# Fourteen products of 64 rows in place of three full ones and a half: a fused attention and MLP layer on one core

## The chip, the cores and the metric

The kernel runs on one core of one Trainium2 chip. The metric is the device time of one execution in microseconds; smaller is better. Of the kernel before there are three timed runs and one profiled execution.

## The reference

The layer computes two branches on the same normalised input, and adds both to the input:

```python
x = A_x                                  # [1, 2048, 448], bfloat16
xn = layernorm(x)
# branch A: linear attention with a feature map, 16 heads of 28
q, k, v = split_heads(xn @ wqkv)         # wqkv [448, 1344]
pq, pk = per_head(q @ w_phi), per_head(k @ w_phi)
phi_q = concat([softmax(pq), softmax(-pq)])
phi_k = concat([softmax(pk), softmax(-pk)])
kv = einsum("bhsf,bhsd->bhfd", phi_k, v);  z = phi_k.sum(over s)
o = (phi_q @ kv) / (phi_q . z + 1e-6)
# branch B: MLP with 1792 hidden features, mish(h) = h * tanh(softplus(h))
return x + o @ wo + mish(xn @ w1 + b1) @ w2
```

What matters here is that the model width is 448, which is three and a half times TensorE's 128 rows.

## The kernel before

The 2048 tokens are 16 tiles of 128, taken in 8 pairs u. For each pair the kernel normalises both tiles (bn_stats and bn_aggr on DVE in `st`, Ln and Exp on ACT, the scaling on POOL or DVE in `xn`) and transposes the result (`xt`, by DMA from SP or by TensorE). Each tile's 448 features give three chunks of 128 rows and one of 64; the two 64-row chunks of a pair share one block, one in rows 0 to 63 and the other in rows 64 to 127. So a transposed pair is 7 blocks in `xnT`.

Every product over the 448 features is built by `pair_part` (L376) for two results at once: part F is six products over 128 rows, three for each result, and part H is two products over 64 rows, one in each half of TensorE's array. F and H are separate steps and either may come first; the two PSUM banks of the pair are held from the first to the second. The units are v and k (8 each, 448 columns), q (2 x 4, 512 columns), f (the first MLP product, 2 x 14, 512 columns), and wo (8, 448 columns, L707, written out in the same way). The second MLP product g (L692) has 1792 rows, which is 14 full chunks, for each of 16 tiles.

Wq and Wk are first multiplied by w_phi: wtq and wtk transpose them on TensorE (L468), wmq and wmk multiply by a block-diagonal matrix `Wbd` (L481) that POOL builds with a mask, and ACT or DVE evicts the results into Wpq and Wpk. These steps run at the start, while the inputs load. TensorE first runs NWARM products on zeros.

After k, ACT takes two exponentials (L518), `kn` normalises them on DVE (L528, L530) and POOL (L532), and `kv` (L553) sums over tokens in column halves of the array. After all eight kv, `kvz` on DVE stores the sums for `nd` (L623), 16 small products of 56 rows in row halves for each tile, whose seven DVE instructions (L639 to L650) give o. `ot` transposes a pair of o by DMA for wo. f is evicted by ACT with the Mish function (L602), q by two exponentials (L588). ACT's function table is loaded with `ACT_TABLE_LOAD` whenever its function set changes.

The order of all steps is one hand-written list, `ORDER`. Each engine runs its own steps in that order, one after the other, and so does each DMA queue: an issue on SP that waits (for example `xt3m` for the normalised pair) holds back every later issue on SP. All buffers and PSUM banks are guarded by semaphores that `Program` derives from what each step reads and writes. A name in ORDER ends in the engine: a for ACT, d for DVE, p for POOL, s for a load issued by SP, m for a transpose by DMA.

Of the kernel before, what the change touches and what calls it, by code (L numbers as in the profile page):

```python
# [19 lines left out]
FC = F // P  # L20
G = 4
GP = 112
# [4 lines left out]
NWARM = 12  # L27
# [122 lines left out]
lx1s lpa lx0a lqta lkts bd lkms lbs lx2s table st1 st0 b1 wtk1d wtk0a lqms xn1p lvts lvms wmk1a xn0p st2 lx4s  # L150
wtq1d xt1d xn2p wmk0a wmq1a st3 wtq0d v1Hd k1H k1F xt0m st4 v1Fd wmq0a xn3p xn4p xt2m k0F v0Ha l1ts k0H k2H
kn1.0 st7 xt3m kn1.1 v0Fa v2Fa v2Ha kn0.1 q0.2H k2F q0.2F kn0.0 xt4m v4Fd st5 xn5p k3F kn2.1 kv1 v4Hd k3H k4F
kv0 k4H kn2.0 xn7d q0.0H q0.1H q0.1F kn3.0 l1ms xt5m q0.0F kn4.1 v3Fd k5F st6 kv2 v3Hd v5Ha xn6p k5H kn4.0 v5Fa
q0.3F xt7m k7H xt6m q0.3H k7F v7Fd kv4 kn3.1 kv3 kn5.1 v6Ha kn5.0 v7Hd v6Fa k6F k6H q1.0H kn7.0 q1.2H kn7.1
q1.0F q1.2F f1.3F l2s kn6.1 f0.7F f1.3H f0.7H kv5 kn6.0 kv7 kv6 f0.1F kvz f0.3F nd2 f1.2H f0.3H f0.1H f1.2F
q1.1F nd3 q1.1H nd1 los q1.3H q1.3F f0.4H f0.4F f0.8F f0.2F f0.5F f0.8H f0.2H f0.5H f1.1H f1.1F f1.4F f0.0F
f1.4H ot1m f0.0H f1.13H nd0 f1.13F f1.5F f1.7F f1.7H f1.6H nd7 f1.6F f1.10F ot0m f1.10H nd6 ot3m f1.5H f0.10H
f0.10F f1.0F nd5 f1.0H f0.6H f0.11H f0.6F f0.11F f1.12F nd4 f1.11H f1.12H nd10 f1.11F f0.13F f0.12F f0.12H ot2m
f0.13H nd8 f0.9H f0.9F f1.8F nd11 nd9 f1.8H wo0H g1 g0 wo0F ot5m wo3F nd14 wo3H nd15 ot7m f1.9H f1.9F g6 g7 g11
ot4m wo5H wo2H nd12 nd13 wo5F g5 wo4F wo2F sto3 g10 ot6m g4 g15 wo7H wo6H wo1H sto0 wo4H g8 wo7F wo6F g13 wo1F  # L160
stt15 g9 sto4 g12 g2 sto5 sto6 g3 sto2 sto1 g14 stt14
# [8 lines left out]
def _kernel(es, nc, A_x, A_wqkv, A_w_phi, A_wo, B_w1, B_b1, B_w2, out):  # L170
# [8 lines left out]
    mask = sb("mask", [GP, 4], FP32)  # L179
    Wraw = sb("Wraw", [GP, G, DH], BF16)  # L180
    Wbd = sb("Wbd", [GP, G, 2, 64], BF16)
# [10 lines left out]
    xn = [sb(f"xn{i}", [P, 2 * D], BF16) for i in range(NXN)]  # L192
    xnT = sb("xnT", [P, NU, 7, P], BF16)
    W1 = sb("W1", [P, 4, F], BF16)
    W2 = sb("W2", [P, FC, D], BF16)
    Wo = sb("Wo", [P, 7, D], BF16)
    Wv = sb("Wv", [P, 4, D], BF16)
    Wqk = [sb("Wq", [P, 4, D], BF16), sb("Wk", [P, 4, D], BF16)]
    Wp = [sb("Wpq", [P, 4, G * P], BF16), sb("Wpk", [P, 4, D], BF16)]
    WT = [sb(f"WT{i}", [GP, 2, G, P], BF16) for i in range(2)]  # L200
    actT = sb("actT", [P, FC, S], BF16)
    zeros = actT[:, 0, 0:TCW]
    NE = 3
# [11 lines left out]
    o_sb = [xn[i][:, :].rearrange("p (i d) -> p i d", i=2) for i in range(2)]  # L215

    def as_t(src):
# [4 lines left out]
    t2 = as_t(phik[0])  # L222


    oT_home = [(Wqk[1], [("Wk", i) for i in range(3)]), (Wqk[0], [("Wq", i) for i in range(3)]),
               (Wv, [("Wv", i) for i in range(3)]), (Wp[1], [("Wp", 1, h) for h in range(2)])]

    def oT_of(u):
        flat = oT_home[u // 2][0][:, :, :].rearrange("p c f -> p (c f)")
        return flat[:, (u % 2) * 7 * P:(u % 2 + 1) * 7 * P]  # L230
# [25 lines left out]
    def load_main(eng, name, dst, src):  # L256
        dma(eng, lambda e: e.dma_start(dst[:, 0:3, :], src[0:384, :].rearrange("(c p) f -> p c f", p=P)),  # L257
            w=[(name, 0)], tag="ld" + name)

    def load_tail(eng, name, dst, src):  # L260
        for i, (lo, hi) in enumerate(HALF):
            dma(eng, lambda e, lo=lo, hi=hi: e.dma_start(dst[lo:hi, 3, :], src[384:448, :]), w=[(name, 1 + i)],  # L262
                tag="ld" + name)

    def rows_of(name):
        return [(name, i) for i in range(3)]

    def load_phi(eng):
        dma(eng, lambda e: e.dma_start(Wraw[:], A_w_phi.rearrange("(g j) d f -> (j d) g f", j=4)), w=[("Wraw",)],
            tag="ldWphi")  # L270
# [4 lines left out]
    def load_w2(eng):  # L275
        dma(eng, lambda e: e.dma_start(W2[:], B_w2.rearrange("(c p) d -> p c d", p=P)), w=[("W2",)], tag="ldW2")

    def load_wo(eng):
        for n, (dst, src) in enumerate((
                (Wo[:, 0:3, :], A_wo[0:384, :].rearrange("(c p) d -> p c d", p=P)),  # L280
                (Wo[:, 4:7, :], A_wo[64:448, :].rearrange("(c p) d -> p c d", p=P)),
                (Wo[0:64, 3, :], A_wo[384:448, :]), (Wo[64:128, 3, :], A_wo[0:64, :]))):
            dma(eng, lambda e, dst=dst, src=src: e.dma_start(dst, src), w=[("Wo", n)], tag="ldWo")

    def table():
# [10 lines left out]
    op("POOL", lambda e: e.memset(mask[:], 1.0), w=[("mask",)])  # L296
    op("POOL", lambda e: e.affine_select(out=mask[:], in_=mask[:], compare_op=ALU.is_ge, fill=0.0, base=0,
                                         channel_multiplier=1, pattern=[[-DH, 4]]),
       r=[("mask",)], w=[("mask",)])
    op("POOL", lambda e: e.affine_select(out=mask[:], in_=mask[:], compare_op=ALU.is_ge, fill=0.0, base=DH - 1,  # L300
                                         channel_multiplier=-1, pattern=[[DH, 4]]),
       r=[("mask",)], w=[("mask",)])
    for i in range(NPH):
        op("POOL", lambda e, i=i: e.memset(v_ext[i][:, :, :, DH:DH + 1], 1.0), w=[("v1", i)])
    op("POOL", lambda e: e.memset(Wbd[:], 0.0), w=[("Wbd0",)])
# [54 lines left out]


    open_ = {}

    def pair_part(key, part, works, r, then):
        if key not in open_:
            open_[key] = take2()
            first = True
        else:
            first = False
        b = open_[key]  # L370

        def f(e):
            for o, par, lhs, rhs in works(b):
                for c in range(3) if part == "F" else (3,):
                    k = (0, P) if part == "F" else HALF[par]
                    ins = e.matmul(o, lhs(c, k), rhs(c, k), start=first and c in (0, 3), stop=not first and c in (2, 3))  # L376
            return ins
        pe(f, r, [pb(b), pb(b + 1)], key + part)
        if not first:
            then(b)  # L380
            free2(b)
# [22 lines left out]
    def ln_pair(u, eng):  # L404
        X = xn[u % NXN]
        a, b = 2 * u, 2 * u + 2
        if eng == "POOL":
            op("POOL", lambda e: e.tensor_tensor(shift[:, a:b], mv[:, a:b, 0], rstd[:, a:b], ALU.mult),
               r=[("mv", a), ("mv", a + 1), ("rstd", u)], w=[("sh", u)], tag=f"sh{u}")
            op("POOL", lambda e: e.tensor_scalar(shift[:, a:b], shift[:, a:b], -1.0, 0.0, op0=ALU.mult, op1=ALU.add),  # L410
               r=[("sh", u)], w=[("sh", u)], tag=f"sj{u}")
        for t in (a, a + 1):
            parts = [(0, D, 0)] if t % 2 == 0 else [(384, D, D), (0, 384, D + 64)]
            for n, (lo, hi, at) in enumerate(parts):
                if eng == "POOL":
                    op("POOL", lambda e, t=t, lo=lo, hi=hi, at=at: e.tensor_scalar(  # L416
                        X[:, at:at + hi - lo], x_all[:, t, lo:hi], rstd[:, t:t + 1], shift[:, t:t + 1],
                        op0=ALU.mult, op1=ALU.add),
                       r=[("x", t), ("sh", u), ("rstd", u)], w=[("xn", u % NXN, t % 2, n)], tag=f"xn{t}.{n}")
                else:  # L420
                    op("DVE", lambda e, t=t, lo=lo, hi=hi, at=at: e.tensor_scalar(  # L421
                        X[:, at:at + hi - lo], x_all[:, t, lo:hi], mv[:, t, 0:1], rstd[:, t:t + 1],
                        op0=ALU.subtract, op1=ALU.mult),
                       r=[("x", t), ("mv", t), ("rstd", u)], w=[("xn", u % NXN, t % 2, n)], tag=f"xn{t}.{n}")
# [12 lines left out]
    def xT(u, eng):  # L437
        i = u % NXN
        if eng == "DMA":
            dma("SP", lambda e: e.dma_start_transpose(xnT[:, u, :, :], xn[i][:, :]),  # L440
                r=[("xn", i, 0, 0), ("xn", i, 1, 0), ("xn", i, 1, 1)], w=[("xnT", u)], tag=f"xTm{u}")
            return
        b = take1()
        pe(lambda e: transpose7(e, b, xn[i]), [("xn", i, 0, 0), ("xn", i, 1, 0), ("xn", i, 1, 1), ("ident",)], [pb(b)],
# [6 lines left out]
    def w_bd():  # L451
        for r in range(2):
            op("POOL", lambda e, r=r: e.tensor_tensor(
                Wbd[:, :, r, 0:QP].rearrange("p g (j f) -> p g j f", f=DH),
                ap_on(Wraw[:, 0, 0:1], [[DH, G], [0, 2], [1, DH]]),
                ap_on(mask[:, 2 * r:2 * r + 1], [[0, G], [1, 2], [0, DH]]), ALU.mult),
               r=[("Wraw",), ("mask",), ("Wbd0",)], w=[("Wbd", r)], tag=f"Wbd{r}")
# [366 lines left out]
```

## Time and profile before

| | us |
|---|---|
| timed runs, median of 3 | 161.92 (161.06 to 162.26) |
| profiled execution | 162.46 |
| its span, first to last instruction | 160.7 |
| TensorE products (PE), busy | 152.4 |
| DVE, busy | 100.9 |
| ACT, busy | 75.6 |
| POOL, busy | 45.5 |

The page gives busy time and share of each engine, the span in 40 slices with the busy share of each in tenths, the clock that TensorE was granted, the DMA engines' share, and the chain of work that ended last. PE is a product on TensorE, PEld a load of its stationary weights, which runs beside products. In the rows of a timeline the columns are start, duration, engine, line, operation, tiles and count, and in brackets the idle time before and what ended it; rows of a PE group also hold the pipeline's tail, so that the start times of neighbours give the pace. The rows of a table of stretches hold the stretch, its length, the busy time (and instructions) of PE, PEld, DVE, ACT and POOL, the granted clock, the DMA engines' share and GB/s. TensorE ran 3.6 us of the first 15 at a clock of 0.53 and all else at about full clock. The DMA moved 12.96 MB in all.

### The profile page before, as it was taken

The page shows a single profiled execution, that of the slowest core. Times are in us where ns is not written, and L with a number is a line of the kernel's source. Part 1 is how long each engine was busy: PE and PEld are TensorE (multiplying, and loading weights), DVE is VectorE, ACT ScalarE, POOL GpSimd, SP SyncE. Part 2 cuts the span into 40 slices and gives each one's busy share as a digit, 9 for nine tenths or more (in the row PEclk, how much of TensorE's full clock was granted, in tenths as well). Part 3 has the DMA queues.
Part 4 walks back from the last instruction along what each step waited for, and adds up shares of the span by engine and source line. Part 5 has one row for each costly group of instructions (what it writes and reads, how often), then busy time and mean ns, then how long its engine had stood idle before and what let it go on. Part 6 is the DMA issues. An engine that isn't in the chain of part 4 may idle for free.

```text
span 160.7 us, 3100 instructions
## 1 busy us (share of the span) xinstructions
PE 152.4 (95%) x1300; PEld 74.5 (46%) x1300; DVE 100.9 (63%) x209; ACT 75.6 (47%) x91; POOL 45.5 (28%) x73
## 2 busy tenths in 40 slices
PE   6659999998999999999999999999999999999993
PEld 2346545453444544434444454454545554555551
DVE  1768799999968168910778589988928811311131
ACT  2355988895939949997668756300100000000000
POOL 6766699959989600000000000000000000000000
PEclk9996999999999999999999999999999999999999
DMA  5998948240498000200030203060070130000502
GB/s 146 284 354 129 183 76 324 40 81 2 70 329 259 8 0 4 57 0 0 4 57 0 57 4 57 0 61 0 2 168 8 23 91 0 0 33 0 225 4 86
DMA packets 21306, 12.96 MB, mean 81 GB/s; under 512 B 14892, under 2 KB 20524, under 8 KB 21292
## 3 DMA queue, kind: packets, MB, share of 16 engines
q1 hardware_dynamic: 20524, 12.39, 30.6%
q10 hardware_dynamic: 768, 0.37, 0.9%
q8 instruction: 10, 0.16, 0.4%
q14 instruction: 4, 0.03, 0.1%
HBM read 7.48 MB, written 1.84 MB: 58 GB/s over the span
## 4 chain that ended last, share of the span: by engine, by line
PE 82%; POOL 5%; DVE 5%; DMA 4%; SPq 2%; issue 1%
PE PS L376 41%; PE PS L692 27%; PE PS L707 7%; POOL phik L532 4%; DMA Wq<-in_A_wqkv_dram 4%; PE PS L623 3%; DVE xn L421 2%; PE PS L553 2%; PE PS L481 1%; DVE Sk L528 1%; POOL xn L416 1%; PE PS L468 1%; SPq L262 1%; DVE v_ext L435 1%; SPq L257 0%
## 5 line engine op out<-in xcount | busy, mean ns | idle before, releaser
L376 PE MATMUL PS<-xnT,W 128*128 128x512 bf16 (+1 forms) x224 | 45.9, 379 | 0.0
L692 PE MATMUL PS<-W,actT 128*128 128x448 bf16 x224 | 43.5, 353 | 0.0
L602 ACT ACTIVATE actT<-PS,b1T 128x1024 bf16<-128x1024 f32 x28 | 30.0, 1112 | 21.3 <-PE PS L376 21.3
L692 PEld LDWEIGHTS PS<-W,actT 128*128 128x128 bf16 x224 | 21.8, 98 | 20.9 <-issue 0.8
L376 PEld LDWEIGHTS PS<-xnT,W 128*128 128x128 bf16 (+1 forms) x224 | 17.5, 97 | 23.4 <-issue 4.9
L532 POOL TENSOR_TENSOR phik<-Ek,rSk 128x896 bf16<-128x896 bf16 x16 | 26.8, 1699 | 2.6 <-DVE rSk L530 2.5
L682 DVE TENSOR_TENSOR x_all<-PS,x_all 128x448 bf16<-128x448 f32 x16 | 9.8, 622 | 25.8 <-PE PS L692 24.6
L528 DVE TENSOR_REDUCE Sk<-Ek 128x32 f32<-128x896 bf16 x16 | 16.8, 1050 | 0.6 <-ACT Ek L518 0.6
L588 ACT ACTIVATE EqT<-PS 128x1024 bf16<-128x1024 f32 x16 | 15.2, 1030 | 0.4 <-PE PS L376 0.2
L518 ACT ACTIVATE Ek<-PS 128x896 bf16<-128x896 f32 x16 | 13.8, 915 | 3.3 <-PE PS L376 3.2
L376 PE MATMUL PS<-xnT,Wpq 128*128 128x512 bf16 (+1 forms) x64 | 13.9, 379 | 0.7 <-DVE v_ext L435 0.7
L639 DVE COPY Sq<-PS 128x16 f32<-128x16 f32 x32 | 4.0, 168 | 16.7 <-PE PS L623 16.5
L376 PE MATMUL PS<-Wpk,xnT 128*128 128x448 bf16 (+1 forms) x64 | 13.0, 356 | 0.0
L376 PE MATMUL PS<-Wv,xnT 128*128 128x448 bf16 (+1 forms) x64 | 12.9, 360 | 0.0
L416 POOL TENSOR_SCALAR xn<-x_all,rstd,shift 128x448 bf16<-128x448 bf16 (+2 forms) x21 | 12.1, 589 | 0.7
L395 DVE BATCH_NORM_STATS2 stats<-x_all 128x6 f32<-128x448 bf16 x16 | 9.5, 596 | 3.3 <-DMA x_all<-in_A_x_dram 3.3
L647 DVE TENSOR_TENSOR Ek<-Ek,phik 128x464 f32<-128x464 f32 x16 | 10.3, 642 | 0.6
L643 DVE TENSOR_TENSOR Ek<-PS,Sq 128x464 f32<-128x464 f32 x16 | 10.3, 642 | 0.5
L650 DVE TENSOR_TENSOR xn<-Ek,rden 128x448 bf16<-128x448 f32 x16 | 10.0, 625 | 0.6
L645 DVE TENSOR_TENSOR phik<-PS,Sq 128x464 f32<-128x464 f32 x16 | 10.1, 631 | 0.0
L376 PEld LDWEIGHTS PS<-xnT,Wpq 128*128 128x128 bf16 (+1 forms) x64 | 5.2, 97 | 7.0 <-DVE v_ext L435 1.1
L376 PEld LDWEIGHTS PS<-Wpk,xnT 128*128 128x128 bf16 (+1 forms) x64 | 5.1, 97 | 6.3 <-issue 2.1
(64 smaller groups left out, 111.7 us busy)
## 6 DMA issues: line engine op xcount, KB each, us to landing
W<-in_B_w_dram SPq DMA_DIRECT2D x1, 1568.0 KB, 8.8
out_dram<-x_all SPq DMA_DIRECT2D x7, 224.0 KB, 2.1
W<-in_B_w_dram SPq DMA_DIRECT2D x1, 1344.0 KB, 6.2
x_all<-in_A_x_dram SPq DMA_DIRECT2D x1, 896.0 KB, 7.3
Wo<-in_A_wo_dram SPq DMA_DIRECT2D x2, 336.0 KB, 9.3
x_all<-in_A_x_dram SPq DMA_DIRECT2D x1, 448.0 KB, 5.4
W<-in_B_w_dram SPq DMA_DIRECT2D x2, 224.0 KB, 4.1
Wk<-in_A_wqkv_dram SPq DMA_DIRECT2D x1, 336.0 KB, 4.4
```

What stands on the lines that cost most here:

```text
L376: ins = e.matmul(o, lhs(c, k), rhs(c, k), start=first and c in (0, 3), stop=not first and c in (2, 3))
L416: op("POOL", lambda e, t=t, lo=lo, hi=hi, at=at: e.tensor_scalar(X[:, at:at + hi - lo], x_all[:, t, lo:hi], rstd[:, t:t + 1], shift[:, t:t ...
L518: op("ACT", lambda e, s=s: e.activation(Ek[i][:, s, :, :], two(b, D), ACT.Exp, scale=1.0 if s == 0 else -1.0), r=[pb(b), pb(b + 1)], w=[(" ...
L528: op("DVE", lambda e: e.tensor_reduce(Sk[i][:, s, :], Eh(), AX.X, ALU.add), r=[("Ek", i, s)], w=[("Sk", i, s)], tag=f"Sk{u}.{s}")
L532: op("POOL", lambda e: e.tensor_tensor(phik[j][:, s, :, :].rearrange("p i (h f) -> p (i h) f", f=DH), Eh(), ap_on(rSk[i][:, s, 0:1], [[1, ...
L588: op("ACT", lambda e, s=s: e.activation(EqT[:, s, g, q * 1024:(q + 1) * 1024], bank(b, 2), ACT.Exp, scale=1.0 if s == 0 else -1.0), r=[pb( ...
L602: op("ACT", lambda e: e.activation(actT[:, fc, q * 1024:(q + 1) * 1024], bank(b, 2), ACT.Mish, bias=b1T[:, fc:fc + 1]), r=[("b1T",), pb(b) ...
L643: op("DVE", lambda e: e.tensor_tensor(tv(t1[i]), num(0), sx(1), ALU.mult), r=[pb(b), pb(b + 1), ("Sq", i, 1)], w=[("t1", i)], tag=f"ta{t}")
L645: op("DVE", lambda e: e.tensor_tensor(tv(t2), num(1), sx(0), ALU.mult), r=[pb(b), pb(b + 1), ("Sq", i, 0)], w=[("t2",)], tag=f"tb{t}")
L647: op("DVE", lambda e: e.tensor_tensor(t1[i], t1[i], t2, ALU.add), r=[("t1", i), ("t2",)], w=[("t1", i)], tag=f"tc{t}")
L692: ins = e.matmul(bank(b)[:, 0:D], actT[:, fc, tok(t)], W2[:, fc, :], start=first and fc == 0, stop=last and fc == FC - 1)
L707: ins = e.matmul(bank(b)[:, 0:D], oT_of(u)[lo:hi, cc * P:(cc + 1) * P], Wo[lo:hi, cc, :], start=first and c in (0, 3), stop=last and c in ...
```

## The change

All products over 448 rows become 14 products of 64 rows, seven for each of the two results, which alternate between the upper and lower half of the array. F and H are one step, `pair_mm`, and the banks are no longer held between parts. To serve both halves, each transposed block now holds the same 64 features of both tiles of a pair, one tile in each half, and every weight (Wv, W1, Wo, Wpq, Wpk) lies in both halves: Wv, W1 and Wo are loaded twice, once into each half, by two DMA steps; Wpk is computed in both halves (56 products over 64-column halves for wmk, 16 before for one copy); Wpq is computed once into Wqn and copied into both halves by four DMAs (`lqs`). Wq is no longer transposed by TensorE but by DMA from DRAM (`ltq`).

Buffers are shared anew: the early weights lie in parts of `actT`, W2 in the places of Ek and phik (so it is loaded after the kv steps), Wo in that of Wpk, o's transposes in those of v_ext, Wv and Wpq. The mask of `Wbd` is built for 128-row windows that cut across heads. ORDER is written anew: among other things five f units come ahead of k6, and W1's two halves are loaded on SP after `lqs`, the second one after `xt4m`. NWARM is 11.

```diff
+K7 = D // 64
-NWARM = 12
+NWARM = 11
...
+    def load_rows(name, dst, src, eng, half):
+        lo, hi = HALF[half]
+        dma(eng, lambda e: e.dma_start(dst[lo:hi, :, :], src.rearrange("(c p) f -> p c f", p=64)), w=[(name, half)],
+            tag="ld" + name)
...
+    def copy_q(eng):
+        for i in range(2):
+            dma(eng, lambda e, d=HALF[i]: e.dma_start(Wp[0][d[0]:d[1], 0:7:2, :], Wqn[0:64, 0:4, :]),
+                r=[("Wqn", c) for c in range(4)] + [("Wqn0",)], w=[("Wp", 0, i)], tag="ldWpq")
+            dma(eng, lambda e, d=HALF[i]: e.dma_start(Wp[0][d[0]:d[1], 1:7:2, :], Wqn[64:128, 0:3, :]),
+                r=[("Wqn", c) for c in range(4)] + [("Wqn0",)], w=[("Wp", 0, 2 + i)], tag="ldWpq")
...
+    def load_wT(h):
+        def part(lo, hi, at, n):
+            dma("SP", lambda e: e.dma_start_transpose(WT[0][:, :, at:at + hi - lo], A_wqkv[lo:hi, 0:NW * P]),
+                w=[("WT", 0, n)], tag="ldWT")
+        if h == 0:
+            part(0, 256, 0, 0)
+        else:
+            part(256, 448, 256, 1)
+            part(384, 448, 448, 2)
...
-    def pair_part(key, part, works, r, then):
-        if key not in open_:
-            open_[key] = take2()
-            first = True
-        else:
-            first = False
-        b = open_[key]
+    def pair_mm(key, works, r, then):
+        b = take2(False)
         def f(e):
-            for o, par, lhs, rhs in works(b):
-                for c in range(3) if part == "F" else (3,):
-                    k = (0, P) if part == "F" else HALF[par]
-                    ins = e.matmul(o, lhs(c, k), rhs(c, k), start=first and c in (0, 3), stop=not first and c in (2, 3))
+            ww = works(b)
+            for c in range(K7):
+                for par, (o, lhs, rhs) in enumerate(ww):
+                    ins = e.matmul(o, lhs(c, HALF[par]), rhs(c, HALF[par]), start=c == 0, stop=c == K7 - 1)
             return ins
...
+lx0a lx1s lk2a lps bd lk1a lk0a table st0 lx2s lbs st1 wtk1d wtk0d wmk3a wmk2a st2 ltq1 b1 ltq0 lv0s xn0p xt0d
+xn1p wmk1a xn2d lv1s wmk0a lx4s wmq1a st3 xt1d xt2d xn3d wmq0d k0 k1 kn0.0 v0a kn0.1 xt3m k2 lqs st4 v2d k3 v1a
+q0.1 xn4p q0.0 l10s q0.2 kn1.1 kn1.0 st6 kv0 xt4m st5 kn2.1 kv1 st7 v3d xn6p l11s xn7p v4d k4 f0.1 f0.2 kn2.0
+kn3.0 xt6m xt7m f0.11 kn4.0 f0.13 xn5d kn3.1 xt5m f0.0 k6 kn4.1 k7 kv3 kv2 kv4 v6a k5 v7a q0.3 kn6.0 v5a q1.1
+kn7.0 kn7.1 q1.2 kn6.1 q1.0 kn5.0 kn5.1 kv7 kv6 kv5 lo0s kvz q1.3 f0.7 nd3 f0.3 f1.2 nd1 f1.9 f0.4 nd0 ot0m
...
```

In ORDER, `l10s` and `l11s` are W1's two halves, `lv0s` and `lv1s` Wv's, `lo0s` and `lo1s` Wo's, `ltq1` and `ltq0` the transposes of Wq, `lqs` the copies of Wpq, and `lk2a`, `lk1a`, `lk0a` the loads of Wk.

## The prediction

> **What bounds the kernel now.** I read the page first (shares, the 40 slices, the chain that ended last), then TensorE's weight loads around a few products, then stretches of the DMA and the clock.
>
> ```profile
> PE 152.4 (95%) x1300; PEld 74.5 (46%) x1300; DVE 100.9 (63%) x209; ACT 75.6 (47%) x91; POOL 45.5 (28%) x73
> ...
> PE   6659999998999999999999999999999999999993
> ...
> ACT  2355988895939949997668756300100000000000
> ...
> PEclk9996999999999999999999999999999999999999
> DMA  5998948240498000200030203060070130000502
> ...
> PE 82%; POOL 5%; DVE 5%; DMA 4%; SPq 2%; issue 1%
> ```
>
> TensorE is full from slice 4 to the end and is 82% of the chain: only what TensorE does, or waits for, counts. The first slices are loads (DMA 9) and the clock falls once (a 6).
>
> Weight loads start with their products, so their start times give the pace:
>
> ```profile
> 64.65 0.10 PEld L376 LDWEIGHTS PS<-xnT,W 64*128 64x128 bf16 x2 [0.42 <-DVE phik L645]
> 64.97 0.98 PEld L376 LDWEIGHTS PS<-xnT,W 128*128 128x128 bf16 x6 [0.23 <-issue]
> 66.24 3.59 PEld L376 LDWEIGHTS PS<-xnT,W 128*128 128x128 bf16 x18 [0.29 <-ACT EqT L588]
> 70.26 0.55 PEld L376 LDWEIGHTS PS<-xnT,W 64*128 64x128 bf16 x8 [0.42 <-issue]
> 71.23 3.57 PEld L376 LDWEIGHTS PS<-xnT,W 128*128 128x128 bf16 x18 [0.42 <-issue]
> 75.22 0.33 PEld L376 LDWEIGHTS PS<-xnT,W 64*128 64x128 bf16 x6 [0.42 <-issue]
> ```
>
> From 70.26 to 71.23 run eight half products (four pairs), from 64.65 to 64.97 two (one pair): 0.97 - 0.32 = 0.65 us for three pairs, **0.216 us a pair**. From 64.97 to 70.26 run 24 full ones, from 71.23 to 75.22 eighteen: 1.30 us for six, again 0.216 each. So a pair of halves costs what one full product costs, and what is left over in each stretch (0.97 - 4 x 0.216 = 0.106; 3.99 - 18 x 0.216 = 0.102) is the price of one **change between whole array and halves: 0.105 us**. At 448 columns a product takes 0.1895 (in the chain, the last 70 of L692 take 13.26).
>
> ```profile
> 39.04 1.47 PE L376 MATMUL PS<-xnT,Wpq 128*128 128x512 bf16 x6 [0.67 <-DVE v_ext L435]
> ...
> 44.39 0.65 PE L553 MATMUL PS<-v_ext,phik 128*56 128x58 bf16 x32 [0.41 <-POOL phik L532]
> ```
>
> These are the only waits after the start, 0.84 and 0.5 us in spacing. A check of the method: 28 f units of 7 x 0.216 (42.3), 8 q (12.1), 16 k and v of 7 x 0.1895 (21.2), 8 wo (10.6), 224 L692 (42.4), 16 nd of 0.22 (3.6), 8 kv of 0.48 (3.9), wmq0 0.45: 136.6. With 52 changes (5.5), the two waits (1.3) and a slow-clock start (0.35) that is 143.7; the first product starts at 14.18, so the end is 157.9. The chain has 158.0.
>
> **The change, part by part.**
>
> *Mode changes.* Reading both orders from the first k or v product on, TensorE changes between whole array, row halves and column halves 52 times before and 11 times after (kv three times in and out, g and wo five). 41 x 0.105 = **-4.3 us**. The 60 units keep their 7 pairs at the pace of a full product; the extra 360 instructions start 4 ns behind their partners in the trace. The two old waits and the slow-clock start go too (-1.65) if nothing replaces them, and wmq0 moves ahead of the products (-0.45).
>
> *The start.* Order now: wtk1, wtk0, wmk3, wmk2, b1, xT0, wmk1, wmk0, wmq1, xT1, xT2, wmq0, k0. x tiles 4 to 7 landed at 9.3 before, behind 1480 KB; now 1432 KB stand ahead, so again 9.3. DVE: st2 to 10.9 (four instructions, 1.44), b1 and xT0 evictions to 11.7, xn2 to 12.6; PE xT2, then wmq0's 16 products of some 133 columns at 0.056 to 14.0. ACT's evictions of wmk (0.5, then 0.92 three times) end at 13.2, behind neither. The clock in this stretch was at half before (below); that would double wmq0's 0.9, bounds 14.0 and 14.9, and I take 14.8: **+0.6**. The Wq transposes now come by DMA straight from DRAM, which no row shows; from SBUF a transpose takes 3.2 us to land (DMA issues, xnT<-xn). SP issues these at about 3 and 5, so they land near 9 (hidden), or at worst one such 3.2 behind all the first loads, which ended near 13 before: 16, and k0 +3. I take hidden, since they are issued ahead of Wv and x_all's last 896 KB.
>
> *W1, the term that decides.* It is loaded twice, 1568 KB (1.606 MB) into each half of the partitions, after the copy of Wpq, by one queue in order. No row has such a load; bounds are
>
> ```profile
> 17.60:18.20 0.60, 0.60 (x7) 0.33 (x5) 0.60 (x1) 0.57 (x3) 0.00 (x0) 1.00 0.94 245
> ...
> 50.00:51.20 1.20, 1.20 (x8) 0.54 (x6) 1.17 (x2) 1.08 (x2) 1.20 (x1) 1.00 1.07 311
> 51.22:51.45 0.23, 0.23 (x3) 0.11 (x2) 0.23 (x2) 0.23 (x1) 0.23 (x1) 1.00 0.61 121
> 24.50:27.00 2.50, 2.50 (x15) 1.22 (x13) 2.40 (x7) 2.50 (x4) 2.50 (x2) 1.00 1.02 400
> ```
>
> (last two columns: DMA share, GB/s). W1's 128-row part moved 400 GB/s. In the first row W1's two 64-row tails end, 245 at a share of 0.94 (261 when full); in the third Wo's 64-row tails end, 121 at 0.61 (198 when full), where the rows just before had 311. So 198 to 261 for a half, and 400 if halves aren't slower at all. I take 230, the middle of the nearer rows: 7.0 us a half. SP: xt3m waits for xn3 (DVE, behind st3, two xT evictions: 16.2), issues to 17.5 (1.22 each), then four issues of lqs (0.58 each); its 917 KB flow from 18.6 for 4.0 us; W1's first half to 29.6; xt4m's transpose, queued behind it, 1.3; W1's second half to 37.9; about 1.0 to landing: **38.9**. f0.1 is wanted at 14.8 + 10 k/v units (13.3) + 3 q (4.5) + kv0, kv1 (1.2) = 33.8. TensorE stands 5.1 us (1 of it already at v4, for xt4m): **+5.1**. Everything behind f0.1 in TensorE's queue waits with it, and ACT for that. What hides W1 now is that it is issued at 15 and 22 and first used at 51; moving five f units ahead of k6 takes that cover off.
>
> The Trainium skill, "SBUF — State Buffer", section "Door 1: The DMA port swizzle", says that 64 partitions reach 8 of the 16 DMA ports and gives 196 GB/s at 1 MiB, some 218 at most. By its figures, an estimate, the second half would land 1 to 3 us later still; the 245 above speaks for a little more than it states, and no run here shows such a load alone.
>
> *Clock.* Before, TensorE was busy 0.94 of 2.30 us just ahead, and then got half its clock for 3.6:
>
> ```profile
> 9.00:11.30 2.30, 0.94 (x18) 0.78 (x16) 1.53 (x5) 1.53 (x4) 1.51 (x3) 1.00 1.11 362
> 11.30:14.90 3.60, 3.60 (x34) 2.88 (x31) 3.21 (x8) 2.43 (x6) 2.11 (x5) 0.53 0.81 165
> ```
>
> A stand of some 4 us should do it again; bounds 0 and 3.6 x 0.47 = 1.7. I take **+1.1**.
>
> *Later waits.* An nd chain holds DVE 3.0 us (from one to the next where they stand back to back); 22 f and 14 nd give TensorE 36 us for 42 of DVE, so o of tile 10 and 11 and its transpose come late for wo5: 0.9. Another 0.6 for small ones like the old two: **+1.5**.
>
> *At nothing, and their cover.* Two more table loads (1.28 each): ACT has about 42 us of work between k0 and kvz, TensorE 44 and the stand; thin, 2 us if gone. Wv's two halves land near 15, first used by v0 at 17.5; W2 in Ek and phik waits for kv and for nd2 ahead of it on SP, lands near 95, used past 104; Wo likewise; copies of q land at 23.5 for q0.1 at 24.1 (cover 0.6). xn in two POOL instructions, not three, saves 0.3 each off the path.
>
> **Sum.** Before: 157.9 to the last product. After: f0.1 at 38.9, then 28 f, 5 q, 6 k/v, 6 kv, 16 nd, 8 wo, 224 L692 and 9 changes (118.3), clock 1.1, waits 1.5: 159.8, **+1.9**. In terms: -4.3 - 0.45 - 1.65 + 0.6 + 5.1 + 1.1 + 1.5 = +1.9. The profiled execution was 162.46 for a span of 160.7 (1.8 outside it, unchanged); it stands 0.5 above the median of the runs, 161.92. So 164.4 on its base, 163.8 on the median's.
>
> **Rivals.**
> 1. *W1 is in time; only the saving is left.* At 341 GB/s, which 17.10 to 17.50 had with tails of both halves mixed, lqs takes 2.7 and the halves 4.7: landing 33.0, before 33.8. No stand, no clock: 33.8 + 118.3 + 1.5 = 153.6, -4.3, **157.6** (to 159.5 with other waits). For it: 64-row tails did run that fast for 0.4 us. Against: the halves here come one after the other.
> 2. *Cancelled out.* Halves at the upper row (261: 3.5 and 6.2 each) land W1 at 36.8, late by 3.0, and a stand that short, cut by work from v4 and k4, keeps the clock: 36.8 + 118.3 + 1.5 = 156.6, -1.3, **160.6** to 163.
> 3. *Wq transposes from DRAM late.* wmq1 and wmq0 stand in TensorE's queue ahead of k0; past 13 each us counts. At 16, and lqs and W1 behind them, +3: **167**. Against: transposes moved 224 KB within 3.2.
> 4. *Halves don't keep pace.* The Trainium skill, "TensorE: Matmul & The Clock Gate", Part 3, "The mechanism", has weight loads overlap running products only in other row groups. By that the load of a half under its own product (95 ns, 420 pairs) would show: +40, **204**. The trace disagrees: in the eight halves at 70.26 pairs come every 0.216.
>
> **Chances.** Forecast 0.5 (own range 162.7 to 166.5), rival 1 0.25, rival 2 0.15, rival 3 0.08, rival 4 0.02. 1% is 1.6 us, about what a measurement here can tell from no change. Faster by more: rival 1, 0.25. Within: rival 2 and the lower edge of the forecast, 0.27. Slower: 0.48. The range leaves out rival 1's best case and the late ends: 157.9 to 167.0.
>
> **What would show it.** Right: weight loads of the k, v, q, f and wo products all 64 rows wide, in pairs every 0.216 or 0.19, without the issue gaps; TensorE idle before the first product with W1, released by the DMA of W, and PEclk below 9 in the slice after; W loads of 1568 KB landing 8 us or more after issue. Wrong: that product starting before 35, loads of W at 300 GB/s or more, or idle before k0 on the DMA that writes actT.

## The result, and the profile after

The changed kernel takes **168.8 us** (median of four runs, 168.53 to 168.93) against 161.5 of the kernel before on the same chip: a ratio of 1.045, 95% interval 1.039 to 1.050. It is slower, as forecast, but by 7.3 us and not by 1.9, and it lies above the forecast's range. The profiled execution is 168.53 with a span of 166.8; before it was 162.46 and 160.7, so the two traces are 6.1 apart.

The page of the changed kernel, the lines that answer to those of before:

```profile
PE 153.0 (92%) x1697; PEld 80.1 (48%) x1697; DVE 100.2 (60%) x214; ACT 76.0 (46%) x91; POOL 40.3 (24%) x61
...
PE   6599999841699999999999999999999999999993
...
PEclk9999999999579999999999999999999999999999
DMA  5999599989900012000038764032006301000213
...
PE 79%; DMA 9%; DVE 4%; ACT 3%; POOL 1%; issue 1%; ACTq 1%; DVEq 0%; POOLq 0%
```

Before, TensorE was full from slice 4 on. Now there is a hole in slices 8 to 10 (4.17 us each: 33 to 46 us), with the clock at 5 and 7 in its last slice and the next one, while the DMA stays at 8 or 9 until the hole ends. The DMA's share of the chain has gone from 4% to 9%. From slice 11 on TensorE is as full as before.

TensorE's products in that stretch (start, duration, engine, line, operation, tiles, count, and the idle time before with what ended it):

```profile
15.84 2.82 PE L421 MATMUL PS<-Wpk,xnT 64*128 64x448 bf16 x28
18.50 1.49 PE L421 MATMUL PS<-Wv,xnT 64*128 64x448 bf16 x14
...
25.45 4.71 PE L421 MATMUL PS<-xnT,Wpq 64*128 64x512 bf16 x42 [0.18 <-issue]
30.09 1.11 PE L606 MATMUL PS<-v_ext,phik 128*56 128x58 bf16 x64
...
35.46 1.50 PE L421 MATMUL PS<-Wv,xnT 64*128 64x448 bf16 x14 [2.82 <-DMA xnT<-xn]
36.78 1.50 PE L421 MATMUL PS<-Wpk,xnT 64*128 64x448 bf16 x14
43.31 10.04 PE L421 MATMUL PS<-xnT,W 64*128 64x512 bf16 x70 [5.03 <-DVE xn L463]
53.17 2.82 PE L421 MATMUL PS<-Wpk,xnT 64*128 64x448 bf16 x28
```

The pace is what the change promised: 28 products of 448 columns, 14 pairs, in 2.66 us (15.84 to 18.50) is 0.19 a pair, and 21 pairs of 512 columns with one mode change take 4.64 (25.45 to 30.09). But v4 stands 2.8 us for the transpose of tile 4 (xt4; "tile" with a number means the pair u here and in what was expected of the runs), f0.1 stands 5.0 more, and the five f units behind it take 9.86 us (43.31 to 53.17) where 35 pairs at 0.216 would take 7.56.

The stretches of the two loads of W1 (length, busy times and counts of PE, PEld, DVE, ACT and POOL, granted clock, DMA share, GB/s), and then those of the clock:

```profile
24.00:32.00 8.00, 7.82 (x130) 4.28 (x128) 7.69 (x18) 7.36 (x9) 6.12 (x6) 1.00 1.06 205
32.00:34.50 2.50, 0.64 (x8) 0.10 (x3) 1.25 (x2) 1.94 (x7) 1.54 (x4) 1.00 1.27 90
34.50:42.30 7.80, 2.83 (x28) 1.51 (x28) 5.13 (x8) 1.73 (x2) 5.22 (x8) 0.93 1.06 210
...
40.00:43.00 3.00, 0.00 (x0) 0.00 (x0) 2.93 (x7) 0.10 (x1) 3.00 (x3) 0.70 1.05 180
43.00:46.00 3.00, 2.69 (x14) 1.21 (x16) 2.58 (x4) 0.00 (x0) 3.00 (x2) 0.50 1.24 189
```

Each half of W1 needs about 8 us at some 205 GB/s, and between them lies the transpose of tile 4, which was issued at 25.73 and landed 9.6 us later because it stood behind the first half. The DMA issues (KB each, median us from issue to landing):

```profile
W<-in_B_w_dram SPq DMA_DIRECT2D x2, 1568.0 KB, 14.5
...
xnT<-xn SPq DMA_TRANSPOSE x5, 8.5
```

and of the line that issues the loads of Wv and W1, the shortest, median and longest time to landing:

```profile
DMA to landing us min/median/max: 4.8/9.3/16.2
```

The transposes took 3.1 before. W1's upper half is issued at 27.02 and lands after the longest of these, 16.2 us, at 43.2; f0.1 starts at 43.31. The wait is written down to "DVE xn L463", the normalisation of tile 5, which f0.1 does not read (it reads the pairs 0 to 3): that instruction only ended last before 43.31. Which of the two it is, is left to the first experiment.

### The profile page after: what moved, and what is told of

It is laid out like the page before. It is cut to its first block, busy times and chain, and to the rows that moved or that the text cites. A ratio compares the mean times of both kernels' runs of the same rounds, so it can differ in the third digit from the quotient of the medians.

```text
span 166.8 us, 3905 instructions
## 1 busy us (share of the span) xinstructions
PE 153.0 (92%) x1697; PEld 80.1 (48%) x1697; DVE 100.2 (60%) x214; ACT 76.0 (46%) x91; POOL 40.3 (24%) x61
## 4 chain that ended last, share of the span: by engine, by line
PE 79%; DMA 9%; DVE 4%; ACT 3%; POOL 1%; issue 1%; ACTq 1%; DVEq 0%; POOLq 0%
PE PS L421 38%; PE PS L741 26%; PE PS L755 6%; DMA xnT<-xn 6%; DMA actT<-in_A_wqkv_dram 3%; ACT Ek L571 3%; PE PS L674 2%; PE PS L527 2%; PE PS L606 2%; DVE Sk L581 2%; PE PS L510 1%; PE PS L472 1%; POOL xn L459 1%; ACTq L293 1%; DVE v_ext L479 1%
## 5 line engine op out<-in xcount | busy, mean ns | idle before, releaser
L421 PE MATMUL PS<-xnT,W 64*128 64x512 bf16 x392 | 46.9, 390 | 5.0 <-DVE xn L463 5.0
L421 PEld LDWEIGHTS PS<-xnT,W 64*128 64x128 bf16 x392 | 19.2, 97 | 26.9 <-DVE xn L463 5.4
L741 PE MATMUL PS<-phik,actT 128*128 128x448 bf16 x128 | 26.8, 352 | 0.0
L741 PEld LDWEIGHTS PS<-phik,actT 128*128 128x128 bf16 x128 | 12.5, 98 | 11.7
L741 PE MATMUL PS<-Ek,actT 128*128 128x448 bf16 x64 | 14.8, 353 | 0.0
L421 PE MATMUL PS<-Wv,xnT 64*128 64x448 bf16 x112 | 11.9, 349 | 2.8 <-DMA xnT<-xn 2.8
L421 PE MATMUL PS<-xnT,Wpq 64*128 64x512 bf16 x112 | 12.8, 376 | 0.2 <-issue 0.2
L421 PE MATMUL PS<-Wpk,xnT 64*128 64x448 bf16 x112 | 11.6, 349 | 0.0
L741 PEld LDWEIGHTS PS<-Ek,actT 128*128 128x128 bf16 x64 | 6.0, 98 | 6.1 <-issue 0.7
L421 PEld LDWEIGHTS PS<-xnT,Wpq 64*128 64x128 bf16 x112 | 5.6, 94 | 6.4 <-issue 0.6
```

Of the source, the lines that this page charges most:

```text
L421: ins = e.matmul(o, lhs(c, HALF[par]), rhs(c, HALF[par]), start=c == 0, stop=c == K7 - 1)
L741: ins = e.matmul(bank(b)[:, 0:D], actT[:, fc, tok(t)], W2_of(fc), start=first and fc == 0, stop=last and fc == FC - 1)
```

## The experiments

Theory A: the time is lost to W1's two half loads, ahead of the early f units. Rivals: B, the loads stand badly in the queue and their rate does not matter; C, f0.1 waits for something else, such as the normalisation that the profile names.

### W1 over all 128 partitions

The edit, shortened (here and below, calls and names are cut down to what matters):

```diff
-    dma_start(W1[lo:hi, :, :], B_w1.rearrange("(c p) f -> p c f", p=64))      # twice, lo:hi = 0:64 and 64:128
+    wide = AP(B_w1, [[F, P], [64 * F, K7 - 1], [1, F]])                        # rows 64c .. 64c+127
+    dma_start(W1[:, 0:K7 - 1, :], wide)
+    dma_start(W1[0:64, K7 - 1, :], B_w1[384:448, :]);  dma_start(W1[64:128, K7 - 1, :], B_w1[0:64, :])
...
-    W1[k[0]:k[1], c, cols]
+    W1[k[0]:k[1], (c - par) % K7, cols]
```

> W1 is loaded with all 128 partitions at once: one DMA of overlapping rows (rows 64c to 64c+127 for c from 0 to 5, so that the upper half of the array gets piece c+1), and two of one half each for the seventh block. The products, their order and the places of the loads in the queue stay. Theory A (the time is lost to the two half loads, each 1.606 MB at about 200 GB/s, 8 us, in one queue with the loads ahead of them): 2.75 MB at the 400 GB/s that two halves together would take are 6.9 us, W1 has landed by 34 to 37 instead of 43.2, unit f0.1 starts there and not at 43.3, the clock does not fall as far, and the time is about 160 to 163. Theory B (the loads are merely issued late, behind the Q projection's loads and around the transpose of tile 4; their rate does not matter): W1 lands at 42 or later and the time stays within 1 us of 168.8. Theory C (f0.1 waits for normalised rows or for a buffer, not for W1): W1 lands earlier but f0.1 starts at 43 all the same, and the time stays at 168.8.

**159.77 us** (159.53 to 160.3), ratio 0.987 (0.982 to 0.991): 9.0 us less than the changed kernel, and 1.3% below the kernel before. Its stretch of the wide load, and its products:

```profile
25.00:30.00 5.00, 5.00 (x70) 2.65 (x72) 4.79 (x13) 3.77 (x5) 3.06 (x2) 1.00 1.03 390
```

```profile
34.00 1.50 PE L431 MATMUL PS<-Wv,xnT 64*128 64x448 bf16 x14 [1.88 <-DMA xnT<-xn]
...
36.65 7.73 PE L431 MATMUL PS<-xnT,W 64*128 64x512 bf16 x70
44.20 2.83 PE L431 MATMUL PS<-Wpk,xnT 64*128 64x448 bf16 x28
```

The same 3.2 MB in rows of the same length now run at 390 GB/s. f0.1 starts at 36.65, 6.7 earlier, right behind k4 and with no wait, and its five units take 7.55 at full clock, 2.3 less. 6.7 + 2.3 = 9.0: the whole of the difference. Up to 1 us of it may be no gain of the load: k0 began at 14.68 here and at 15.84 in the changed kernel, which the edit doesn't touch, and the transpose of tile 4, which v4 and behind it f0.1 hang on here, was issued 1.0 earlier (24.77 for 25.73). B and C fall; the row "DVE xn" was a wrong name for the wait. Three of the runs below put other names beside it, and in each f0.1 starts within 0.1 us of the landing of W1's upper half (43.27 after 43.21 in the first run with the ACT queue, 44.05 after 43.95 with products on zeros, 43.47 after 43.4 in the tile-4 order without the wide load).

### The five early f units put later

```diff
-... v4d k4 f0.1 f0.2 kn2.0 kn3.0 xt6m xt7m f0.11 kn4.0 f0.13 xn5d kn3.1 xt5m f0.0 k6 ... q1.3 f0.7
+... v4d k4 kn2.0 kn3.0 xt6m xt7m kn4.0 xn5d kn3.1 xt5m k6 ... q1.3 f0.1 f0.2 f0.11 f0.13 f0.0 f0.7
```

> The five units of the W1 projection that the changed order starts early (f0.1 f0.2 f0.11 f0.13 f0.0) are put behind the last unit of the Q projection, ahead of f0.7; loads and products stay as they are. Theory A: nothing wants W1 before about 60 us, so the stand of 5.2 us before f0.1 and the 2.3 us that the fallen clock cost go; the wait of v4 for the transpose of tile 4 (2.8 us) may stay or be followed by waits for the transposes that follow: 160 to 163. Theory B (the five units only cover waits that are there anyway for transposes and normalised rows of tiles 5 to 7): the stand only moves to kn3, kn4 or k6, and the time falls by less than 3 us, 166 to 169.

169.05 us, ratio 1.044 (1.038 to 1.051): no gain, and A in that form was wrong. Products behind k4:

```profile
44.16 5.01 PE L421 MATMUL PS<-Wpk,xnT 64*128 64x448 bf16 x28 [6.65 <-DMA xnT<-xn]
```

Now it is k6 that stands, 6.7 us, for transposes of tiles 5 to 7, which stand behind W1's upper half in SP's queue. The slow loads do not only keep back who reads W1: 16 us of DMA in the middle of the queue keep back whatever comes next. The early f units only decide who waits.

### The upper half on the ACT queue, twice

```diff
-q0.1 xn4p q0.0 l10s q0.2 ... xn6p l11s xn7p
+q0.1 xn4p q0.0 l10s l11a q0.2 ... xn6p xn7p                    # first run
+... lqs st4 l11a v2d k3 v1a q0.1 xn4p q0.0 l10s q0.2 ...       # second run
```

> The load of W1 into the upper half is issued from the ACT queue beside the load of the lower half from the SP queue, instead of behind it. Theory A1 (each half load is bound by what its 64 partitions can take): the two run at once at 350 to 400 GB/s together, both land by 34 to 36, f0.1 starts there, 160 to 163. Theory A2 (both halves together share about 200 to 250 GB/s because something else binds them): they land at 40 or later, and the time is 166 to 169. In a sentence of its own: the Trainium skill, SBUF — State Buffer, says of two DMAs to the two halves at once that it brings some 6 per cent only, which is A2.

168.02 us, ratio 1.039 (1.033 to 1.044), which looks like A2, but the run does not test it:

```profile
29.81 0.65 ACTq L278 DMA_DIRECT2D W<-in_B_w_dram  x1
```

ACT came to the issue only at 29.81, when the lower half had 3 us to go; the upper half's first data came at 33.65, after the lower half's last at 32.9, so the two loads never met. I misread that at first as two queues worked off strictly in order, and the expectation of the early wide load below still says so. So the issue was moved up:

> The run with the upper half on the ACT queue told nothing of two loads at once, since ACT came to that issue only at 29.81, when the lower half was nearly done. Here the issue stands behind st4 in ACT's order, at about 23.5, so that both half loads of the changed kernel flow at the same time from about 25.7 on. Theory A1 (200 GB/s is what the 64 partitions of one half take, whichever queue): together 350 to 400 GB/s, both landed by 33 to 35, the transpose of tile 4 with them, f0.1 at about 36 to 37, 160 to 162. Theory A2 (two loads into different halves share about 200 GB/s): the last of them lands at 41 or later, 166 to 169.

167.95 us, ratio 1.039 (1.035 to 1.044). The stretches with one half load alone, with the upper half's data beginning at 29, and with both:

```profile
25.00:29.00 4.00, 2.53 (x18) 1.26 (x20) 3.83 (x11) 0.96 (x2) 2.90 (x2) 0.83 1.06 201
28.00:30.00 2.00, 2.00 (x12) 0.79 (x10) 1.93 (x5) 1.43 (x2) 0.11 (x1) 0.50 1.03 202
30.00:32.00 2.00, 2.00 (x16) 1.01 (x14) 1.17 (x4) 1.06 (x2) 1.59 (x1) 0.73 1.04 324
```

On the rate the run gives both answers: 201 GB/s for one half, no more in the first microsecond of two (29 to 30, in the row at 202), then 324 for two halves together, well over A2's 200 and short of A1's 350 to 400. On the time A1 is wrong. ACT's load, issued at 22.25, moved nothing until 29; from then the two shared, from 33 the upper half went on alone, and the transpose of tile 4 landed behind both: v4 stood 5.7 us, f0.1 came at 45.5. Why the second queue's load began so late stays open. The Trainium skill, "SBUF — State Buffer", section "Can I just issue two DMAs to hit both halves?", gives two such loads 6% over one; the row at 202 agrees, the 324 against 201 says more.

### Products on zeros between k4 and f0.1

```diff
-... v4d k4 f0.1
+... v4d k4 fill f0.1            # fill: 20 products zeros x zeros, 512 columns
```

> Twenty products on zeros are put on TensorE between k4 and f0.1, while it stands for W1 anyway; nothing reads them. If the clock of 0.5 to 0.8 after the stand is the price of the stand, the five units after f0.1 take 7.6 us instead of 9.9 and the time falls by 2 to 2.5 us, to about 166.5. If the clock falls for another reason (a budget of work over time), the units stay slow or are slower, and the time is 168.5 or more.

167.44 us, ratio 1.033 (1.029 to 1.037): 1.4 less than the changed kernel.

```profile
37.25 4.49 PE L827 MATMUL PS<-actT 128*128 128x512 bf16 x20
44.05 7.73 PE L421 MATMUL PS<-xnT,W 64*128 64x512 bf16 x70 [2.30 <-DVE rSk L583]
51.60 2.83 PE L421 MATMUL PS<-Wpk,xnT 64*128 64x448 bf16 x28
```

With TensorE kept busy the five units take 7.55 and not 9.86: the stand's price in clock is **2.3 us**. The gain is less because f0.1 came 0.7 later here (44.05 for 43.31): W1's last data were in at 41.4, 0.9 earlier than in the changed kernel, but the landing came 2.6 after them and not 0.9. Why is not shown.

### More mode changes

```diff
+    if full:                     # the 28 f units
+        e.matmul(bank(b)[:, 0:8], ident[:, :], ident[:, 0:8], start=True, stop=True)
     for c in range(K7):
```

> At the head of each of the 28 units of the W1 projection one product over all 128 rows is put, 8 columns wide, into a bank whose first product over 64 rows then starts it anew: two more changes of the array's mode for each unit, 56 in all, and 28 products of 8 columns. If a change costs the 0.105 us that the trace of before shows, 56 of them add 5.9 us and the small products 28 times up to 0.02: 174 to 176. If a change costs next to nothing (so that the 41 changes that the new order saves are worth nothing and its gain, if any, is elsewhere), the time stays at 168.8 to 169.8.

175.28 us, ratio 1.086 (1.079 to 1.093): 6.5 more than the changed kernel, for 56 changes and 28 small products; expected 5.9 to 6.5. In the profiled execution f0.1 also came 0.8 later than in the changed kernel's, which the added products do not explain.

```profile
88.82 0.18 PE L420 MATMUL PS<-ident 128*128 128x8 bf16 x1
88.93 1.69 PE L423 MATMUL PS<-xnT,W 64*128 64x512 bf16 x14
90.55 0.18 PE L420 MATMUL PS<-ident 128*128 128x8 bf16 x1
```

A unit comes every 1.73 us instead of 7 x 0.216 = 1.51: 0.22 for two changes and the small product. The 0.105 that was read from the left-overs of two short stretches in the trace of before holds. The change's own saving, 4.3 us, is this price times the 41 changes counted in the two orders; it was not measured apart.

### Where else the wide load could stand

All four runs below have W1 over all 128 partitions as in the first experiment.

```diff
 early, on ACT:       ... wmk0a lx4s wmq1a l10a l11a st3 ...
 behind tile 4:       ... kv0 xt4m l10s l11s st5 ...
 cut in two:          ... q0.0 l10s(blocks 0-2) ... kv0 xt4m l11s(blocks 3-6) st5 ...
 tile 4 first:        ... wmq0d st4 xn4p k0 k1 ... k2 lqs xt4m v2d ... q0.0 l10s l11s ...
```

> As the run with W1 over all 128 partitions, and its three loads are issued from the ACT queue right behind wmq1a, ahead of the transposes of tiles 3 and 4 and of the Q projection's loads, instead of from the SP queue behind them. Theory A, with what the last runs showed (the DMA engines work off what was issued in order, also across two queues): W1 has landed before it is wanted, v4 waits for nothing of W1, but 3.2 MB at 390 GB/s, 8 us, now stand ahead of the transpose of tile 3 (wanted at 20) and of Wq (wanted at 24), and a wait of 2 to 4 us arises there, which f0.1 and the transpose of tile 4 no longer have: 158 to 162, about the 159.8 of the wide load. If the two queues did not hold each other up: no wait at all, f0.1 at 34, 157.

166.72 us, ratio 1.033 (1.026 to 1.040).

```profile
29.29 2.80 PE L431 MATMUL PS<-Wpk,xnT 64*128 64x448 bf16 x14 [6.68 <-DMA xnT<-xn]
```

W1 lands early, and k3 stands 6.7 us for the transpose of tile 3, and pays half the clock for it (14 products in 2.56 us for 1.33). A wait did arise, longer than the 2 to 4 us expected.

> As the run with W1 over all 128 partitions, and the loads of W1 are issued behind the transpose of tile 4 and not ahead of it. Theory A: the wait of v4 for that transpose (1.9 us in that run) goes, W1 flows from about 26.5 for 8 us and lands at 35, f0.1 could start at 34.8 when nothing stands before it, so it starts at 35 to 35.5 instead of 36.65: 158 to 159. Rival: the transposes of tiles 5 to 7 now stand behind W1's last piece and kn3 or k6 wait for them: 159.5 to 162.

165.61 us, median of four runs from 163.67 to 167.14; the ratio, 1.019 (1.009 to 1.029), counts only the lower two of them.

```profile
39.24 9.29 PE L431 MATMUL PS<-xnT,W 64*128 64x512 bf16 x70 [2.79 <-DMA W<-in_B_w_dram]
```

v4's wait is gone, but tile 4 is normalised only at 25.5, and of W1 behind it the last data come at 38.6 and the landing at 39.1, not at 35: a stand of 2.8 and a slower clock.

> As the run with W1 over all 128 partitions, but its wide load is cut in two: blocks 0 to 2 (1.38 MB) where it stood, ahead of the transpose of tile 4, blocks 3 to 5 and the two short loads of the seventh block behind that transpose. Theory A: the first part flows from 23.5 to about 27, the transpose lands by about 29 and v4 (wanted at 32) no longer waits 1.9 us for it, the second part and the short loads need 3.5 + 2.3 us and land at 34.5 to 35.5, f0.1 starts at 35 to 35.5 instead of 36.65: 158 to 159. Rival: as in the run with W1 wholly behind the transpose, tile 4 is normalised late (25.5), the second part starts behind it and lands at 37 or later, f0.1 waits and the clock falls after that wait: 160 to 163.

161.33 us, median of 13 runs from 159.04 to 164.65; the ratio, 0.989 (0.986 to 0.993), counts only the lower seven of them. The profiled one, at 164.65, shows f0.1 standing 3.2 us for W1's last part and the slower clock behind it. That the other long ones stood there too is likely and not shown.

> As the run with W1 over all 128 partitions; in the order, tile 4 is normalised before k0 (st4 and xn4p ahead of k0, where POOL is idle for 8.9 us), its transpose is issued right behind the Q projection's loads, and W1's wide load and its two short ones follow without a gap. Theory A: the transpose lands at about 26 and nothing waits for it, W1 flows from about 25 for 8 to 10 us and lands at 34 to 35, f0.1 starts at 34.7 to 35.5 instead of 36.65: 157.5 to 158.8. Rival: the normalisation of tile 4 delays k0's or kn0's work on DVE and POOL, or W1 lands later than v4 and k4 end and f0.1 waits again with a slower clock behind it: 160 to 163.

160.47 us, ratio 0.993 (0.990 to 0.996). f0.1 waits 1.4 us for W1 and starts at 38.0; v2 waits 1.5 for ACT, which the earlier statistics of tile 4 put back. None of the four comes below the first placement, W1 ahead of the transpose of tile 4. The early one and the one behind tile 4 are slower; the other two, at 0.989 and 0.993 against 0.987 with intervals that overlap, can't be told from it by their ratios.

### The tile-4 order without the wide load

> The changed kernel with that same change of order alone: the transpose of tile 4 ahead of W1, the lower half's load and behind it at once the upper half's, both of 64 partitions as in the changed kernel. Theory A: v4's wait of 2.8 us for the transpose goes, but f0.1 waits for W1 as before: two halves of 8 us in one stretch from about 25 land at 41, so f0.1 starts at 41 instead of 43.3, 165.5 to 167. If v4's wait were a loss of its own beside W1's, 3 us and more would go: 164 to 165.5. If W1's landing did not bind f0.1: below 163.

168.24 us, ratio 1.042 (1.038 to 1.046). Both half loads in one stretch:

```profile
26.00:34.00 8.00, 8.00 (x130) 4.14 (x128) 7.57 (x18) 7.14 (x9) 5.22 (x4) 0.97 1.03 212
34.00:41.00 7.00, 3.79 (x42) 1.75 (x36) 5.45 (x7) 4.18 (x10) 5.07 (x10) 0.94 1.06 206
```

v4 no longer waits for its transpose, and next to nothing is won (0.6 us): f0.1 starts at 43.47. Fifteen us of W1 are here in two rows at 206 to 212 GB/s, with a DMA share above 1. The landing I expected, 41, was 2 too early, as the loads began at 25.5 and ended at 42.8. So v4's 2.8 us in the changed kernel were no loss of their own: whatever went ahead of f0.1 was paid for by W1's landing.

### Both halves from one DMA for each piece

```diff
-    dma_start(W1[lo:hi, :, :], B_w1.rearrange("(c p) f -> p c f", p=64))
+    for c in pieces:
+        dma_start(W1[:, c, :], AP(B_w1, 64 * c * F, [[0, 2], [F, 64], [1, F]]))
```

> W1 keeps the changed kernel's layout (the same 448 rows in both halves) and its products stay word for word; each of its seven pieces of 64 rows is loaded by one DMA that writes both halves (the source is read twice by a stride of zero), four DMAs in the place of the lower half's load and three in the place of the upper half's. Same bytes and the same 3584 bytes a row as in the changed kernel. Theory A1 (a load that writes only 64 partitions runs at 200 GB/s, one that writes 128 at 390): W1 lands by 36 to 37, f0.1 starts there, 159.5 to 161.5, as in the run with the wide load. Theory A2 (what made the wide load fast was that rows were not read twice, or its one large transfer): about 200 GB/s still, W1 at 42, 167 to 169.

214.91 us, ratio 1.332 (1.323 to 1.341): neither theory.

```profile
30.00:34.00 4.00, 1.93 (x50) 0.99 (x42) 2.31 (x5) 3.23 (x9) 2.88 (x5) 1.00 0.13 50
```

A share of 0.13 is 2 of 16 DMA engines: the pattern with an outer dimension of 2 was spread over two engines only, 50 GB/s. The run says nothing of halves against whole. What it was to tell apart, two others do. In the first experiment, too, every row of W1 is read twice. In the run with the wide load cut in two, its two pieces of 1.38 MB, each smaller than a half load, moved 387 GB/s (27 to 28) and 398 to 405 (32 to 34). So neither the double reading nor the size made the half loads slow; the 64 partitions are what is left. The Trainium skill, "DMA: Bandwidth & Descriptors", section "Why a DMA increments its semaphore by 16 and not by 1", has the engines' number be the largest up to 16 that divides both sides' slowest dimensions; for 2 and 128 that is 2, and the trace agrees.

## Why the prediction was wrong

The sign and the mechanism were right: a change that saves 4.3 us on TensorE, and a stand before f0.1, for W1, that costs more. The size was wrong, and the step that failed is **"W1, the term that decides"**.

| step | forecast | measured |
|---|---|---|
| mode changes | -4.3, 0.105 each | 0.11 each (28 units with two more) |
| W1 begins to flow | 22.6 | 24.0 |
| a half of W1 | 7.0 us at 230 GB/s | 8.1 and 7.7 us |
| between the halves | 1.3 | 2.5 |
| last data to landing | 1.0 | 0.9 |
| f0.1 starts | 38.9 | 43.3 |
| clock after the stand | +1.1 | +2.3 |
| waits behind f0.1 | +1.5 | none |
| last product ends | 159.8 | 163.8 |

*The rate.* For a load no row showed, I had bounds of 198 and 261 GB/s and took their middle. Neither row showed one half alone: all 41 data packets of the first have the size of W1's rows, those of the third of Wo's, and both times the tails of two halves stood one behind the other. Nor does division by the share give the full rate, since the share is 1.06 at 205 GB/s and 1.03 at 390. That the lower row was nearer is luck. By their own 1.606 MB the two halves ran at 198 and 209 GB/s and cost 1.8 us more than forecast. The rule that I set beside it, 196 GB/s in the Trainium skill, "SBUF — State Buffer", "Door 1: The DMA port swizzle", was nearer than my choice, and I turned it down for the row that fitted it least; the traces, 201 to 212, lie 3 to 8% above it.

*What stood around it.* W1 began 1.4 later. Of that, 1.1 stands at the transpose of tile 3, issued at 17.32 and not at 16.2, as DVE normalised the tile later, and 0.3 in the copies (5.4 us from their first issue to W1's first data, 5.1 put). k0, too, came 1.0 late, at 15.84 (the runs have it anywhere from 14.4 to 17.1): the 32 products of wmk ahead of it took 1.85 us here and 1.05 in the run with the five units put later, so the half pace that the forecast allowed wmq0 fell on others. That is not W1's delay: in that run, with k0 at 14.76, the transpose was issued at 17.06 and W1 began at 23.7. The gap with the transpose was 2.5 and not 1.3. Together: 1.4 + 1.8 + 1.2 - 0.1 = 4.3 of the 4.4 that f0.1 is late.

*Clock.* The upper bound was taken from one slow stretch of 3.6 us at 0.53, 1.7. Here the clock was at 0.5 from 41.2 to 48.0, twice as long, and the 4.7 us of it in which products ran cost 2.3, as the products on zeros show. The length of the stand doesn't give that of the slow stretch: 6.8 us also followed stands of 3.2 us (load cut in two) and 6.7 (load early), and 3.4 us a stand of 2.8 (load behind tile 4).

*Later waits.* None came: from f0.1 to the last product the wide run takes 118.2 us (36.65 to 154.9) where the prediction had 118.3 without waits. The 3.0 us of a nd chain on DVE was right (3.0 from one to the next here too), but behind f0.1 TensorE shows no wait at all; the step from it to 0.9 at wo5 was not worked out. The term hid part of the two misses: 4.4 + 1.2 - 1.5 = 4.1, and 1.9 + 4.1 = 6.0 of the 6.1 between the traces.

*Edits at nothing.* Most stood: Wq's transposes by DMA, Wv's and Wo's halves and W2's late load show in no wait of TensorE. One did not: the copies of Wpq, put at 23.5 with a cover of 0.6. They landed at about 25.4. q0.1 waited 0.2 us for them in the changed kernel, where k0 was late, and 0.8 to 2.7 in four runs with k0 at 14.4 to 15.3 (the first, the five units later, W1 behind tile 4, the second with the ACT queue); in the changed kernel W1's stand covers it. Rival 1, W1 in time, is nearly what the first experiment made of the kernel: there f0.1 comes at 36.65, 2.9 after that rival's 33.8, and 157.6 plus 2.9 is within 0.7 of the 159.8 measured. Rivals 3 and 4 did not occur; half pairs came every 0.216.

*The range.* The lower row, 198 GB/s, alone gives 8.1 a half, 2.2 more for both, and 166.0: inside. The start, the gap and the clock (1.4 + 1.2 + 1.2, less the 1.5 of waits) then make 168.3, outside it. The clock's bound was 1.7, too low; the other two had none, though all lie on the one path with W1.

## What to carry to other kernels

When a change moves or doubles a load, price it by a row of the trace whose destination it shares (here 64 partitions), not by the average of rows that are near in time, and where no row shows it alone, let the range reach past the slowest. Then follow what is queued behind that load, since the five f units, the transposes and the copies all waited in turn. A layout that wants the same weights in both halves can still be loaded over all 128 partitions, if the second half takes its rows in a shifted order and the products follow it: here, for W1, this is the difference between 4.5% slower and 1.3% faster. Read the name in a wait as the last that ended, and check whether the waiting instruction reads it at all.

## What the runs showed of the hardware

- A DMA share of 1.0 is no sign of full rate: loads into 64 partitions had shares of 1.03 to 1.06 at 201 to 212 GB/s, a load into 128 had 1.03 at 390.
- A stand of TensorE costs clock from a length that is not fixed: after 1.9 us (wide load, before v4) and 2.8 us (the changed kernel, before v4) it stayed at full, after 2.0 us (tile-4 order, before v2) it fell to 0.5, and after 2.8 us (wide load behind tile 4, before f0.1) the five units took 9.1 us for 7.55. The slow stretches lasted about 3.4 us or about 6.8, whatever the stand. The Trainium skill, "TensorE: Matmul & The Clock Gate", Part 1, puts the idle window at about 3.4 us and calls it free-running, not tied to the kernel's start; the 2.0 us here is shorter.
- A load issued on a second queue while the first queue has a long one in flight may move nothing for 6.7 us (issued at 22.25, first data at 29; in the first run with the ACT queue, issued at 29.81, first data at 33.65).
